# Linear attention with RMS norm and a mish feed-forward on one core: the start in halves and pairs, activation tables loaded at named places, steps placed anew

## The chip, the core and the metric

The kernel runs on one core of one Trainium2 chip. A core has a matrix engine (TensorE, PE in the profile; its weight loads are PEld), VectorE (DVE), ScalarE (ACT), GpSimd (POOL) and SyncE (SP), which work side by side, each on its own queue of instructions in order, and 16 DMA engines. SP issues nearly all loads, POOL most stores. The metric is the time of the whole program on the device, in microseconds (us), lower being better.

## The reference

q, k and v have 8 batches, 8 heads, 576 rows and 64 columns per head; x has 4608 rows of 512 columns.

```
kv  = einsum('bhsd,bhde->...', k, v)      # k^T v, 64 x 64 for each batch and head
out = einsum('bhsd,bhde->bhse', q, kv)
x   = out / sqrt(mean(out*out, -1) + 1e-6) * g_norm     # per row and head
h   = x @ w_in                             # 512 -> 2048
g   = h * tanh(log(1 + exp(h)))            # mish
res = g @ w_out                            # 2048 -> 512, fp32
```

w_in and w_out come in as 64-bit floats.

## The kernel before, in words

*Words and splits.* A unit j of w_in (two blocks of 256 columns, all 512 rows, 1 MB as 64-bit words) is loaded as pairs of 32-bit words by two DMAs, turned to fp32 by one ScalarE instruction (`scale`, L225) and three VectorE instructions (`join`, L220 to L222), and split into a high part, rounded to fp32r (`blocks`, ScalarE, L214), and a low part, the rest (VectorE, L215). A product of two such numbers takes three matmuls: high x high, high x low, low x high. x is split the same way. Each unit later gives differences of its blocks (`diff`), which are split too (`sums`) and stored (`store`), for a scheme with 7 block products in place of 8 (`group`, from L646).

*Tiles and slots.* The 4608 rows are nine tiles of 512. Part 1 makes h and g tile by tile, and stores g in DRAM; part 2 multiplies g by w_out. The order of part 1 is a row of numbered slots. A slot holds one product on TensorE, and behind it the steps that are due. Tile 0 has slots 0 to 31 and is multiplied in plain form (`whole_group`, L703: slots 0 to 3 use the first half of x's 512 columns, x0.0, kept in pages pa0 and pa1, slots 4 to 7 the second half, x0.1, in pb0 and pb1; two units of w_in each eight slots). Tiles 1 and 2 have slots 32 to 87, 12 matmuls of 256 columns each (L725); from slot 88 two tiles go together, 6 matmuls of 512 columns a slot (L735). Part 2 starts at about 434 us (L1256, L1106, L1111).

*Steps and places.* All else is in named steps: `w2.join` is the join of unit 2, `x0.1.rstd` the inverse root of tile 0's second half, `k5.v1` the load of v for the second half of the heads of batch 5, `k5.mul1` its k^T v product, `k5.keep1` the copy of that out of PSUM, `f1.0.0` a form of tile 1's x. The table `WHEN` gives each step its place as a number: a whole number t means behind the product of slot t, numbers below 0 come before slot 0, in their order. Nothing else sets the order: every engine's queue gets its instructions in that order, and waits are added where data or a buffer demand them. A step's place thus sets its order on its engines, not its time.

*Tile 0's attention* (the start). `kv.a` and `kv.b` load k and v of batch 0 (heads 0 to 3, heads 4 to 7), `rows.a` and `rows.b` the rows of q for the same heads, `rows.c` those of tile 1. Then for u = 0, 1 (four heads each): TensorE turns q (`transpose`, L484), ScalarE copies it out (`turned`, L495, L497), TensorE projects it on k^T v (`project`, L511), ScalarE squares (`square`, L517, L520), TensorE sums the squares over the head's 64 columns (`sums`, L534), ScalarE takes Ln and Exp (`rstd`, L547, L548), VectorE multiplies (`normalize`, L571), and `whole.u` splits the result. Each step handles two pairs of heads (1024 elements a partition) in one go, in one two-bank PSUM tile for u = 0. The first k^T v (`kv_first_product`, L389) writes the results of all pairs of heads straight, so it uses two of the four 64 x 64 quadrants of the array; later batches (`kv_product`, L400) use four, and `kv_keep` then swaps halves of the odd pairs back with two VectorE copies.

*Buffers.* w0, w4 and w7 share one room (w64): the load of w4 waits until w0's join has read it, and what follows on SP waits with it. v has one buffer per half batch (vm), k two: a load of v waits until the product before it has ended. wd (the differences) and x2 (PSUM) have one buffer as well.

*Tables.* ScalarE evaluates Ln, Exp and Mish from a loaded table; a function that is not in the current one makes the compiler put an ACT_TABLE_LOAD before it. `table.exp` (a set that holds Ln and Exp) and `table.mish` are explicit loads; `WHEN` has them at 139.787 and 110.923, so at the start Ln and Exp load a table each. For tiles 1 to 8, `rstd` loads the joint set itself, and the next mish loads its own.

Of the kernel before, what the change touches and what calls it, by code (L numbers as in the profile page):

```python
# [8 lines left out]
F32 = mybir.dt.float32  # L9
# [15 lines left out]
    "kv.a": -58.068, "constants": -56.889, "rows.a": -56.704, "w1.load": -56.033, "kv.mul.a": -55.141, "kv.b": -54.793,  # L25
# [98 lines left out]
def linear_attention_rms_mish_ffn(  # L124
# [140 lines left out]
    def weight_in(j, place):  # L265
# [9 lines left out]
        def scale():  # L275
            st["x"] = ring(j - (NF2 - 2), F32, True)[:, 0:PAGE] if j >= NF2 - 2 else page(f"wfa{j}", F32, True)
            scale_words(st["x"], st["w"])

        def join():
            join_words(st["x"], st["w"])  # L280
# [1074 lines left out]
```

## Time and profile before

| What | Value |
|---|---|
| three timed runs, median (lowest to highest) | 794.69 us (794.43 to 795.37) |
| the profiled execution's own time | 794.12 us |
| its span, first to last instruction | 792.3 us |
| TensorE busy | 772.8 us (98%) |
| VectorE busy | 601.9 us (76%) |
| ScalarE busy | 461.4 us (58%) |
| HBM read and written | 105.64 MB and 58.20 MB |

In the views of the trace, a row of the timeline gives start and duration in us, engine, line, operation, output and inputs, a count, and in brackets how long the engine was idle before it and what it waited for. `x72` at an fp32 matmul of the program counts its records, two for each. A row of the windows gives a stretch, its length, for each engine the busy time and in brackets the number of instructions that began in it (TensorE, its weight loads, VectorE, ScalarE, GpSimd), the granted clock of TensorE, the mean busy share of the DMA engines, and the GB/s that they moved. Matmuls are pipelined and their ends are modelled.

### The profile page before, as it was taken

What the parts mean: (1) busy time and instruction counts of PE and PEld (TensorE: products, weight loads), DVE (VectorE), ACT (ScalarE), POOL (GpSimd) and SP (SyncE); (2) the same over time, 40 slices, a digit from 0 to 9 for tenths busy, and PEclk for the clock granted to TensorE, in tenths of its full rate; (3) what the DMA queues carried; (4) which work ended last, traced back from release to release, by engine and by line L of the source; (5) the groups of instructions that cost most, each with busy time, mean ns of one, the idle gap of its engine ahead of it and who ended that gap; (6) DMA issues with size and microseconds to landing.
All of it is one profiled execution on the core that took longest, in us unless ns stands there. A gap on an engine that the chain in (4) does not pass through costs nothing.

```text
span 792.3 us, 13807 instructions
## 1 busy us (share of the span) xinstructions
PE 772.8 (98%) x5456; PEld 654.8 (83%) x5456; DVE 601.9 (76%) x713; ACT 461.4 (58%) x661; POOL 112.3 (14%) x179
## 2 busy tenths in 40 slices
PE   5799999999999999999999999999999999999997
PEld 4477899898878777888888988888888888888886
DVE  1888859488776986876467988888888888888885
ACT  4878566757666786566567644444444444444442
POOL 1013324232332323212111000000000000000000
PEclk9999999999999999999999999999999999999999
DMA  9997788789897768776847924444444444444412
GB/s 275 280 329 238 267 263 297 254 280 329 292 339 253 256 233 294 248 267 232 281 157 244 328 81 149 138 140 138 141 138 137 136 136 133 134 133 133 134 27 54
DMA packets 97969, 164.76 MB, mean 208 GB/s; under 512 B 15728, under 2 KB 62960, under 8 KB 97904
## 3 DMA queue, kind: packets, MB, share of 16 engines
q1 hardware_dynamic: 84304, 115.56, 46.5%
q0 software_dynamic: 13504, 48.24, 16.2%
q8 instruction: 43, 0.70, 0.4%
q14 instruction: 22, 0.18, 0.1%
q10 hardware_dynamic: 96, 0.07, 0.0%
HBM read 105.64 MB, written 58.20 MB: 207 GB/s over the span
## 4 chain that ended last, share of the span: by engine, by line
PE 92%; DMA 2%; DVE 2%; SPq 1%; ACT 1%; issue 1%; DVEq 0%
PE a L735 16%; PE a L1106 16%; PE bc L1106 12%; PE bc L735 12%; PE a L1111 8%; PE bc L1111 6%; PE a L725 6%; PE bc L725 4%; PE q L1256 3%; PE x L511 2%; PE bc L703 2%; PE a L703 2%; PE s L400 2%; SPq L434 1%; PE ss L541 1%; DMA vm<-in_v_dram 1%
## 5 line engine op out<-in xcount | busy, mean ns | idle before, releaser
L770 DVE TENSOR_TENSOR ula<-bc,ula 128x512 f32<-128x512 f32 x32 | 22.0, 686 | 39.6 <-ACT ur L665 15.4
L211 ACT ACTIVATE ur<-ur 128x1024 f32<-128x1024 f32 x32 | 33.9, 1059 | 25.3 <-DVE ur L770 25.1
L472 POOL COPY qs<-qs 32x1024 f32<-32x1024 f32 x28 | 33.0, 1180 | 43.4 <-DMA qs<-in_q_dram 39.6
L735 PE MATMUL a<-wfa,wfb 128*128 128x512 f32 x144 | 36.9, 391 | 0.0
L735 PE MATMUL bc<-wfa,tr 128*128 128x512 f32 x144 | 36.7, 390 | 0.0
L735 PE MATMUL bc<-wfc,wfb 128*128 128x512 f32 x144 | 36.7, 390 | 0.0
L214 ACT CAST wfc<-wfb 128x1024 fp32r<-128x1024 f32 x23 | 24.0, 1050 | 20.9 <-PE a L1111 11.6
L214 ACT CAST wfa<-g 128x1024 fp32r<-128x1024 f32 (+1 forms) x24 | 23.8, 998 | 19.4 <-PE a L1111 7.8
L215 DVE TENSOR_TENSOR wfa<-g,wfa 128x1024 fp32r<-128x1024 f32 (+1 forms) x24 | 27.5, 1154 | 9.1 <-ACT wfa L214 9.1
L665 ACT COPY ur<-a 128x512 f32<-128x512 f32 x32 | 18.8, 586 | 26.7 <-PE a L735 20.5
L735 PE MATMUL a<-pc,wfb 128*128 128x512 f32 x96 | 33.8, 393 | 0.1
L735 PE MATMUL a<-wfc,tr 128*128 128x512 f32 x96 | 33.8, 393 | 0.0
L735 PE MATMUL bc<-pa,wfb 128*128 128x512 f32 x96 | 33.7, 392 | 0.0
L735 PE MATMUL a<-pb,tr 128*128 128x512 f32 x96 | 33.7, 392 | 0.0
L214 ACT CAST wfa<-wfb 128x1024 fp32r<-128x1024 f32 x19 | 19.9, 1052 | 21.5 <-PE a L1111 15.5
L735 PEld LDWEIGHTS bc<-wfa,tr 128*128 128x128 f32 x144 | 26.9, 188 | 6.4 <-issue 0.8
L735 PEld LDWEIGHTS a<-wfa,wfb 128*128 128x128 f32 x144 | 26.8, 188 | 6.5 <-ACT tr L214 0.8
L211 ACT ACTIVATE ula<-ula 128x512 f32<-128x512 f32 x32 | 20.2, 631 | 19.9 <-DVE ula L770 19.8
L735 PEld LDWEIGHTS bc<-wfc,wfb 128*128 128x128 f32 x144 | 26.9, 188 | 5.7
L1161 DVE TENSOR_TENSOR ur<-ow 128x1024 f32<-128x1024 f32 x16 | 19.6, 1225 | 14.4 <-ACT ow L1158 14.3
L215 DVE TENSOR_TENSOR wfa<-wfb,wfa 128x1024 fp32r<-128x1024 f32 x19 | 23.1, 1221 | 8.9 <-ACT wfa L214 8.9
L770 DVE TENSOR_TENSOR ur<-bc,ur 128x512 f32<-128x512 f32 x32 | 21.9, 684 | 9.7 <-ACT ula L211 4.2
(574 smaller groups left out, 2479.0 us busy)
## 6 DMA issues: line engine op xcount, KB each, us to landing
gp<-ur POOLq DMA_DIRECT2D x24, 512.0 KB, 4.9
g<-gp SPq DMA_DIRECT2D x12, 1024.0 KB
wfb<-gp SPq DMA_DIRECT2D x12, 1024.0 KB
w<-in_moe_w_out_dram SPq DMA_DIRECT2D x16, 512.0 KB
km<-in_k_dram SPq DMA_DIRECT2D x14, 576.0 KB
vm<-in_v_dram SPq DMA_DIRECT2D x14, 576.0 KB
gp<-ula POOLq DMA_DIRECT2D x24, 256.0 KB, 3.9
gp<-ulb POOLq DMA_DIRECT2D x24, 256.0 KB, 3.7
```

The costliest lines, as they stand in the source:

```text
L211: nc.scalar.activation(o, i, AF.Mish)
L214: nc.scalar.copy(hi, src)
L215: nc.vector.tensor_sub(lo, src, hi.bitcast(F32))
L472: nc.gpsimd.tensor_copy(t[(i + 1) * R:(i + 2) * R, :, 0:R], t[i * R:(i + 1) * R, :, R:])
L703: nc.tensor.matmul(banks[m], w[:, a, kc, :], xf[b][:, kc], start=r == kc == s == 0, stop=(r == kc == 1 and s == 2), skip_group_check=True,)
L725: nc.tensor.matmul(bank[:, jj * TH:(jj + 1) * TH], w[:, a, kc, :], xf[b][:, kc], start=first and jj == kc == s == 0, stop=(kc == 1 and s = ...
L735: nc.tensor.matmul(bank, w[:, a, kc, :], xf[b][:, kc], start=first and kc == s == 0, stop=(kc == 1 and s == 2), skip_group_check=True,)
L770: nc.vector.tensor_add(o, bank_view(st, block, bank), o)
L1106: nc.tensor.matmul(halves(bank), gf[0][:, c], wo_form(c, right), start=first and c == 0, stop=False, skip_group_check=True,)
L1111: nc.tensor.matmul(halves(bank)[:, 0], gf[1][:, c], wo_form(c, right)[:, 0], start=False, stop=c == NF2 - 1, skip_group_check=True)
L1161: nc.vector.tensor_add(st["o"].rearrange("p r (c n) -> p (r c) n", c=2), a[:, :, 0], a[:, :, 1])
L1256: nc.tensor.matmul(banks[b][:, h], gf[a][:, c], wo_form(2 * n + c, right)[:, d], start=n == c == s == h == 0, stop=last_one, skip_group_ch ...
```

## The change

The start is cut finer and every step has a new place.

- Units 0, 1 and 2 of w_in are scaled, joined and split in halves (one of two column blocks each), so each of these steps is two; a half needs one of the unit's two DMAs.
- Tile 0's attention goes by pairs of heads: every step but rstd is there twice (512 elements a partition). Projections use the PSUM banks bc, which rotate; high and low parts are steps of their own. rstd does Ln, Exp for the first pair, then Ln, Exp for the second.
- The first k^T v uses `kv_product`, four quadrants, and `kv_keep` with its two VectorE copies.
- The joint Ln/Exp table is loaded by the first instruction on ScalarE; mish's table is loaded at the end of x0.1's rstd and at the end of the rstd of each of tiles 1 to 8. The steps table.exp and table.mish are gone.
- `WHEN` is new throughout. On SP, the order at the start was kv.a, rows.a, w1, kv.b, rows.b, w0, w2, k1.k0, k1.v0, w4, w3, k1.k1, rows.c; it becomes kv.a, rows.a, w1, w0, rows.b, kv.b, w2, k1.k0, k1.v0, w4, w3, rows.c, w5, k1.k1.

The diff, cut to its core:

```diff
 WHEN = {
...
-    "k5.mul0": 70.827, "k5.v1": 74.729, "k5.mul1": 81.43, "k6.mul0": 85.133, "k6.v1": 88.135, "k6.mul1": 90.167,
-    "k4.mul0": 56.221, "k4.mul1": 62.614, "k3.mul0": 39.547, "k3.mul1": 44.249, "table.mish": 110.923, "table.exp": 139.787,
+    "k5.mul0": 78.799, "k5.v1": 78.831, "k5.mul1": 82.324, "k6.mul0": 87.671, "k6.v1": 89.911, "k6.mul1": 91.127,
+    "k4.mul0": 58.613, "k4.mul1": 62.687, "k3.mul0": 40.104, "k3.mul1": 44.815,
+    "rows.a": -54.973, "w1.load": -52.565, "w0.load": -50.279, "rows.b": -49.677, "kv.b": -49.025, "w2.load": -47.673,
+    "x0.0.square0": -46.31, "w1.scale1": -42.097, "w0.scale0": -40.175, "x0.0.project1": -39.243, "x0.0.square1": -37.584,
+    "kv.mul.b": -28.683, "x0.1.project0": -19.47, "w2.scale1": -15.726, "w0.blocks1": -14.997, "w2.blocks0": -12.839,
+    "x0.1.rstd": -11.645, "x0.1.high0": -10.975, "x0.1.low1": -4.102, "k1.mul0": 3.676, "x1.0.transpose": 9.14,
...
-        def scale():
+        def scale(h=None):
+            if "x" not in st:
...
+            scale_words(st["x"][:, half_of(h)], st["w"][:, half_of(h)])
...
-    def kv_first_product(n):
...
-    def kv_first_keep(n):
-        nc.scalar.copy(kvt[0][:, n], kvps[:, 0, n, :])
...
+    def root(r, mean):
+        nc.scalar.activation(r, mean, AF.Ln, bias=eps, scale=1.0 / D)
+        nc.scalar.activation(r, r, AF.Exp, scale=-0.5)
+
+    def first_steps(u):
...
+        def turned(a):
+            if "q" not in st:
+                st["q"] = turned_q if u else att.tile([P, 2, T], F32, name="fh")
+            nc.scalar.copy(st["q"][:, a], st["x2"][:, a])
+
+        def project(a):
+            st["x"][a] = bank_new("bc")
+            for o in range(2):
+                nc.tensor.matmul(st["x"][a][half(o)], kvt[0][half(o), 2 * u + a], st["q"][half(o), a], start=True, stop=True)
...
+        def rstd():
+            for a in range(2):
+                root(st["s"][:, a], st["ss"][a])
+            if u == 1:
+                nc.scalar.preload_act_table_set("mish")
...
+        def high(a):
+            nc.scalar.copy(two(WHOLE[u][0])[:, a], x_part(0, u)[:, a])
+
+        def low(a):
+            hi, lo = (two(name)[:, a] for name in WHOLE[u])
+            nc.vector.tensor_sub(lo, x_part(0, u)[:, a], hi.bitcast(F32))
...
             nc.scalar.preload_act_table_set("natural_log_exp_and_others")
-            nc.scalar.activation(r, ss[j], AF.Ln, bias=eps, scale=1.0 / D)
-            nc.scalar.activation(r, r, AF.Exp, scale=-0.5)
+            root(r, ss[j])
+            nc.scalar.preload_act_table_set("mish")
...
     def k_product(b, n):
-        kt, vt = (staged.pop((name, b, n)) for name in "kv")
-        staged[b, n] = kv_product(b, n, [(kt[:, a], vt[:, a]) for a in range(2)])
+        if b == 0:
+            ts = [[kv0[name][:, hp] if hp + 1 < NKC else kv0[name, NKC] for name in "kv"] for hp in (2 * n, 2 * n + 1)]
+        else:
...
+        staged[b, n] = kv_product(b, n, ts)
...
+    nc.scalar.preload_act_table_set("natural_log_exp_and_others")
     for name, f in begin:
```

In this cut the entries of `WHEN` stand regrouped; all of them have new numbers.

More of the change, by code (lines that the diff above doesn't have):

```diff
@@ L24 @@
 WHEN = {
-    "kv.a": -58.068, "constants": -56.889, "rows.a": -56.704, "w1.load": -56.033, "kv.mul.a": -55.141, "kv.b": -54.793,
[93 rows of a table removed]
+    "constants": -56.889, "kv.a": -55.729, "rows.a": -54.973, "kv.mul.a": -53.46, "x0.0.transpose1": -53.308,
[98 rows of a table added]
 }
@@ L273, in load, with half_of, join @@
             st["w"] = load_words(place(), srcs, 2)
-        def scale():
[L276 to L280, printed above, removed]
+        def half_of(h):
+            return slice(None) if h is None else slice(h * FORM, (h + 1) * FORM)
+        def scale(h=None):
+            if "x" not in st:
+                st["x"] = ring(j - (NF2 - 2), F32, True)[:, 0:PAGE] if j >= NF2 - 2 else page(f"wfa{j}", F32, True)
+            scale_words(st["x"][:, half_of(h)], st["w"][:, half_of(h)])
+        def join(h=None):
+            join_words(st["x"][:, half_of(h)], st["w"][:, half_of(h)])
         def parts(t, src):
@@ L284, in parts, with blocks @@
             split(hi, lo, src)
-        def blocks():
-            wb[j] = wfp.tile([P, 4 * FORM], F32R, name=f"wfb{j}")
-            parts(forms(wb[j]), st["x"].rearrange("p (b n) -> p b n", b=4))
+        def blocks(h=None):
+            if j not in wb:
+                wb[j] = wfp.tile([P, 4 * FORM], F32R, name=f"wfb{j}")
+            n = slice(0, 4) if h is None else slice(2 * h, 2 * h + 2)
+            parts(forms(wb[j])[:, n], st["x"].rearrange("p (b n) -> p b n", b=4)[:, n])
         def differences():
@@ L412, in kv_keep @@
         if b < T32:
-            nc.scalar.copy(kvx[:, n], odd)
+            if b:
+                nc.scalar.copy(kvx[:, n], odd)
             for o in range(2):
@@ L454, in linear_attention_rms_mish_ffn, with transpose, square, sums @@
     SQUARES = {SINGLE + 1: ("xa", "xh")}
+    def root(r, mean):
+        nc.scalar.activation(r, mean, AF.Ln, bias=eps, scale=1.0 / D)
+        nc.scalar.activation(r, r, AF.Exp, scale=-0.5)
+    def first_steps(u):
+        st = {"ps": [None] * 2, "x": [None] * 2, "ss": [None] * 2}
+        def transpose(a):
+            if "x2" not in st:
+                st["x2"] = ps_t.tile([P, 2, T], F32, name="x2")
+            h = 4 * u + 2 * a
+            for c in range(TR):
+                nc.tensor.transpose(st["x2"][:, a, c * P:(c + 1) * P], rows[0][:, c, h * D:(h + 2) * D], ident)
+        def turned(a):
[6 more added lines that the diff above has]
+                nc.tensor.matmul(st["x"][a][half(o)], kvt[0][half(o), 2 * u + a], st["q"][half(o), a], start=True, stop=True)
+        def square(a):
+            if "s" not in st:
+                st["s"] = att.tile([P, 2, T], F32, name=("fa", "fh")[u])
+            nc.scalar.square(st["s"][:, a], st["x"][a])
+        def sums(a):
+            st["ss"][a] = bank_new("a") if u == 0 else ps_t.tile([P, T], F32, name="ss") if a == 0 else kvps.rearrange("p b n d -> p (b n d)")
+            nc.tensor.matmul(st["ss"][a], ones, st["s"][:, a], start=True, stop=True)
+        def rstd():
[3 more added lines that the diff above has]
+                nc.scalar.preload_act_table_set("mish")
+        def normalize(a):
+            nc.vector.scalar_tensor_tensor(x_part(0, u)[:, a], st["x"][a], gcol, st["s"][:, a], ALU.mult, ALU.mult)
+        def high(a):
[3 more added lines that the diff above has]
+            nc.vector.tensor_sub(lo, x_part(0, u)[:, a], hi.bitcast(F32))
+        return {f.__name__: f for f in (transpose, turned, project, square, sums, rstd, normalize, high, low)}
     def unit_steps(j, u):
@@ L475, in transpose @@
             if j < T32:
-                if j == 0 and u == 1:
-                    ps = [ps_t.tile([P, T], F32, name="ss"), bank_new("bc")]
-                else:
-                    x2 = ps_t.tile([P, 2, T], F32, name="x2")
-                    ps = [x2[:, a] for a in range(2)]
+                st["ps"] = ps_t.tile([P, 2, T], F32, name="x2")
                 for a in range(2):
@@ L483, in transpose @@
                     for c in range(TR):
-                        nc.tensor.transpose(ps[a][:, c * P:(c + 1) * P], rows[j][:, c, h * D:(h + 2) * D], ident)
-                st["ps"] = ps if j == 0 and u == 1 else x2
+                        nc.tensor.transpose(st["ps"][:, a, c * P:(c + 1) * P], rows[j][:, c, h * D:(h + 2) * D], ident)
                 return
@@ L491, in turned @@
         def turned():
-            t = st["q"] = turned_q if j == 0 and u == 1 else att.tile([P, 2, T], F32, name="fh")
-            if j == 0 and u == 1:
-                for a in range(2):
-                    nc.scalar.copy(t[:, a], st["ps"][a])
-            else:
-                nc.scalar.copy(t, st["ps"])
-        def project():
-            if j == 0 and u == 1:
-                st["x"] = [bank_new("bc") for _ in range(2)]
-            else:
-                x2 = st["x2"] = ps_t.tile([P, 2, T], F32, name="x2")
-                st["x"] = [x2[:, a] for a in range(2)]
+            st["q"] = att.tile([P, 2, T], F32, name="fh")
+            nc.scalar.copy(st["q"], st["ps"])
+        def project():
+            st["x"] = ps_t.tile([P, 2, T], F32, name="x2")
             for b, _, c in segments(j):
@@ L510, in project @@
                         r = half(o, turned)
-                        nc.tensor.matmul(st["x"][a][half(o), c], kv[r], st["q"][r, a, c], start=True, stop=True)
+                        nc.tensor.matmul(st["x"][half(o), a, c], kv[r], st["q"][r, a, c], start=True, stop=True)
         def square():
-            st["s"] = spare(j, SQUARES.get(j, ("fa", "fh"))[u])
-            sq[j, u] = st["s"]
-            if "x2" in st:
-                nc.scalar.square(st["s"], st["x2"])
-            else:
-                for a in range(2):
-                    nc.scalar.square(st["s"][:, a], st["x"][a])
+            sq[j, u] = spare(j, SQUARES.get(j, ("fa", "fh"))[u])
+            nc.scalar.square(sq[j, u], st["x"])
         def scaled():
@@ L524, in scaled @@
             if j <= T32:
-                nc.scalar.activation(o, st["x2"], AF.Identity, scale=gcol)
+                nc.scalar.activation(o, st["x"], AF.Identity, scale=gcol)
             else:
-                nc.vector.tensor_scalar(o, st["x2"], gcol, None, ALU.mult)
+                nc.vector.tensor_scalar(o, st["x"], gcol, None, ALU.mult)
         def sums():
-            if j == 0:
-                st["ss"] = []
-                for a in range(2):
-                    ps = bank_new("a") if u == 0 else ps_t.tile([P, T], F32, name="ss") if a == 0 else kvps.rearrange("p b n d -> p (b n d)")
-                    nc.tensor.matmul(ps, ones, st["s"][:, a], start=True, stop=True)
-                    st["ss"].append(ps)
-                return
             ss[j] = ps_t.tile([P, T], F32, name="ss")
@@ L543, in rstd @@
         def rstd():
-            if j == 0:
-                r = st["r"] = st["s"]
-                for a in range(2):
-                    nc.scalar.activation(r[:, a], st["ss"][a], AF.Ln, bias=eps, scale=1.0 / D)
-                nc.scalar.activation(r, r, AF.Exp, scale=-0.5)
-                return
             r = st["r"] = att.tile([P, T], F32, name="fl")
             nc.scalar.preload_act_table_set("natural_log_exp_and_others")
-            nc.scalar.activation(r, ss[j], AF.Ln, bias=eps, scale=1.0 / D)
-            nc.scalar.activation(r, r, AF.Exp, scale=-0.5)
+            root(r, ss[j])
+            nc.scalar.preload_act_table_set("mish")
         def keep():
@@ L616, in x_form @@
             nc.scalar.copy(hi, src)
-    def x_whole(r):
-        split(*(two(name) for name in WHOLE[r]), x_part(0, r))
     def bank_new(name):
@@ L804, in k_product @@
     def k_product(b, n):
-        kt, vt = (staged.pop((name, b, n)) for name in "kv")
-        staged[b, n] = kv_product(b, n, [(kt[:, a], vt[:, a]) for a in range(2)])
+        if b == 0:
+            ts = [[kv0[name][:, hp] if hp + 1 < NKC else kv0[name, NKC] for name in "kv"] for hp in (2 * n, 2 * n + 1)]
+        else:
+            kt, vt = (staged.pop((name, b, n)) for name in "kv")
+            ts = [(kt[:, a], vt[:, a]) for a in range(2)]
+        staged[b, n] = kv_product(b, n, ts)
     def k_keep(b, n):
@@ L849, in linear_attention_rms_mish_ffn @@
     t1 = start(1)
-    begin = (
-        ("table.exp", lambda: nc.scalar.preload_act_table_set("natural_log_exp_and_others")),
+    firsts = [first_steps(u) for u in range(2)]
+    begin = [
         ("w0.load", None), ("rows.a", rows_first), ("kv.a", kv_rooms), ("w1.load", None), ("rows.b", rows_second),
@@ L854, in linear_attention_rms_mish_ffn @@
         ("w4.load", None), ("k1.k0", None), ("k1.v0", None),
-        ("w0.scale", None), ("w0.join", None), ("x0.0.transpose", None), ("x0.0.turned", None), ("w0.blocks", None),
-        ("kv.mul.a", lambda: kv_first_product(first)), ("kv.keep.a", lambda: kv_first_keep(first)),
-        ("w1.scale", None), ("x0.0.project", None), ("x0.0.square", None), ("w1.join", None),
-        ("x0.1.transpose", None), ("x0.0.sums", None), ("x0.1.turned", None), ("w1.blocks", None),
-        ("x0.0.rstd", None), ("kv.mul.b", lambda: kv_first_product(rest)), ("kv.keep.b", lambda: kv_first_keep(rest)),
-        ("x0.0.normalize", None), ("x0.1.project", None), ("w2.scale", None), ("whole.0", lambda: x_whole(0)),
-        ("x0.1.square", None), ("w3.scale", None), ("rows.c", rows_next),
-    )
+        ("kv.mul.a", lambda: k_product(0, 0)), ("kv.keep.a", lambda: k_keep(0, 0)),
+    ]
+    FIRST_STEPS = ("transpose", "turned", "project", "square", "sums", "rstd", "normalize", "high", "low")
+    begin += [(f"x0.0.{n}{a}", None) for n in FIRST_STEPS[:4] for a in range(2)]
+    begin += [(f"w0.{n}{h}", None) for n in ("scale", "join", "blocks") for h in range(2)]
+    begin += [("kv.mul.b", lambda: k_product(0, 1)), ("kv.keep.b", lambda: k_keep(0, 1))]
+    begin += [(f"x0.0.{n}{a}", None) for n in FIRST_STEPS[4:] for a in range(2) if n != "rstd"]
+    begin.insert(len(begin) - 6, ("x0.0.rstd", None))
+    begin += [(f"x0.1.{n}{a}", None) for n in FIRST_STEPS[:4] for a in range(2)]
+    begin += [(f"w1.{n}{h}", None) for n in ("scale", "join", "blocks") for h in range(2)]
+    begin += [(f"w2.scale{h}", None) for h in range(2)] + [("w3.scale", None), ("rows.c", rows_next)]
     early = {name: n - len(begin) for n, (name, _) in enumerate(begin)}
+    nc.scalar.preload_act_table_set("natural_log_exp_and_others")
     for name, f in begin:
@@ L866, in linear_attention_rms_mish_ffn @@
             step(name, early[name], f)
[L867 to L875 removed]
+    for u in range(2):
+        for n, name in enumerate(FIRST_STEPS):
+            for a in range(2) if name != "rstd" else ("",):
+                key = f"x0.{u}.{name}{a}"
+                step(key, early.get(key, 0.01 + 0.01 * n), lambda u=u, name=name, a=a: firsts[u][name](*(() if a == "" else (a,))))
     STEPS = ("load", "scale", "join", "blocks", "diff", "sums", "store")
[L878 removed]
+    made = {0: (-80, -25, -24, -20), 1: (), 2: (0, 0, 0.5, 0.6), 3: (0, 0, 3, 5), 4: (0, 6, 6.1, 8), 5: (1, 9, 9.1, 11), 6: (4, 13, 13.1, 15), 7: (8, 16, 16.1, 18)}
     for j in range(NF2):
[L880 removed]
+        t = (1.5, 21, 23, 25, t1 + 6, t1 + 8, t1 + 13, t1 + 15)[j]
         for n, name in enumerate(STEPS):
[L882 to L886 removed]
+            for h in range(2) if j < 3 and 0 < n < 4 else (None,):
+                key = f"w{j}.{name}" + ("" if h is None else str(h))
+                when = early[key] if key in early else made[j][n] if n < 4 else (t, t + 1, t + 0.5)[n - 4]
+                step(key, when, lambda j=j, n=n, h=h: conv[j][n](*(() if h is None else (h,))))
     for b, t, loads, made in (
```

28 lines of the change are left out of this document (1 added, 27 removed), and 191 rows, old and new, of the table WHEN.

## The prediction

> **What bounds the kernel now.** I read the page first, for the share of each engine, then the waits of TensorE, then the windows and the order of time of the first 45 us.
>
> ```profile
> span 792.3 us, 13807 instructions
> PE 772.8 (98%) x5456; PEld 654.8 (83%) x5456; DVE 601.9 (76%) x713; ACT 461.4 (58%) x661; POOL 112.3 (14%) x179
> PE   5799999999999999999999999999999999999997
> ```
>
> TensorE is busy for 98% of the span; its idle time lies in the first two of the 40 slices and at the very end. Its waits after the first product of the feed-forward part (28 to 50 us), and then all from 50 to 440 us (from 440 us on the view is empty), are these:
>
> ```profile
> PE x L484 <- DMA qs<-in_q_dram: 1.1, 1, 1.1
> PE a L703 <- ACT wfb L214: 0.9, 1, 0.9
> PE a L703 <- DVE pb L215: 0.5, 1, 0.5
> PE a L703 <- DVE wfb L215: 0.5, 1, 0.5
> ```
> ```profile
> PE s L400 <- DMA vm<-in_v_dram: 0.8, 1, 0.8
> ```
>
> So the work on TensorE behind the first product is fixed, and the change can win only by starting that work sooner and by taking out these waits, some 3.8 us of them. The rows of the start, in order of time, and four of the chain of waits (start, us):
>
> ```profile
> 6.42 4.09 PE L389 MATMUL s<-wfb,wfb 64*64 64x64 f32 x72 [6.42 <-DMA wfb<-in_v_dram]
> ...
> 12.86 1.14 ACT L225 ACTIVATE wfa<-wfb 128x1024 f32<-128x1024 f32 x1 [0.28 <-DMA wfb<-in_moe_w_in_dram]
> 14.76 1.23 DVE L221 SCALAR_TENSOR_TENSOR wfa<-wfb,wfa 128x1024 uint32<-128x1024 uint32 x1
> ...
> 21.83 0.59 ACT L495 COPY wfa<-ss 128x512 f32<-128x512 f32 x1
> ...
> 22.47 1.93 PE L511 MATMUL bc<-wfa,kv 64*64 64x512 f32 x8 [1.46 <-ACT wfa L495]
> ...
> 26.38 1.02 PE L534 MATMUL s<-fh,ones 128*128 128x512 f32 x2
> ...
> 27.25 0.92 SPq L234 DMA_DIRECT2D w<-in_moe_w_in_dram  x2
> ...
> 28.31 0.73 PE L703 MATMUL a<-pa,wfb 128*128 128x512 f32 x2 [0.91 <-ACT wfb L214]
> ...
> 29.57 2.56 PE L703 MATMUL a<-pa,wfb 128*128 128x512 f32 x10 [0.52 <-DVE wfb L215]
> ...
> 37.05 2.79 PE L703 MATMUL a<-pb,wfb 128*128 128x512 f32 x11 [0.54 <-DVE pb L215]
> ...
> 39.69 0.48 DVE L415 COPY kv<-ss 64x64 f32<-64x64 f32 x2
> ```
> ```profile
> 45.37 0.77 PE x L484 x5
> ...
> 73.93 2.72 PE a L703 x12
> ...
> 86.25 1.43 PE a L725 x12
> ...
> 175.80 7.42 DMA vm<-in_v_dram
> ```
>
> The first tile's attention ends on TensorE at 26.38 + 1.02 = 27.4 us. The first product starts at 28.31 and stalls until 29.57, since w_in's first unit is converted whole and late. The second half of the tile (slot 4, which reads pb) runs from 37.05, one matmul earlier in effect, so I count it from 36.8. The transposes of tile 1 wait for its q rows until 45.37 (45.3 below).
>
> **The change, part by part.** Sums are made against the profiled run: 794.12 us with its span of 792.3; the median of the three timed runs is 794.69, so 0.57 is added at the end.
>
> *DMA order.* These rows give the rates of all DMA (the last figure, GB/s) and the sizes:
>
> ```profile
> 0.00:10.00 10.00, 3.58 (x67) 3.61 (x69) 0.00 (x0) 1.28 (x1) 2.62 (x15) 1.00 0.85 232
> 10.00:20.00 10.00, 7.68 (x103) 4.61 (x101) 3.14 (x3) 7.61 (x9) 0.00 (x0) 1.00 1.10 318
> 25.00:30.00 5.00, 3.15 (x8) 1.36 (x9) 4.97 (x5) 4.65 (x6) 0.00 (x0) 1.00 0.53 173
> 30.00:35.00 5.00, 5.00 (x90) 4.00 (x89) 3.98 (x5) 3.50 (x5) 0.00 (x0) 1.00 1.06 350
> ```
> ```profile
> wfb<-in_moe_w_in_dram SPq DMA_DIRECT2D x10, 512.0 KB
> wfb<-in_q_dram SPq DMA_DIRECT2D x8, 128.0 KB
> wfb<-in_k_dram SPq DMA_DIRECT2D x1, 576.0 KB
> wfb<-in_k_dram SPq DMA_DIRECT2D x1, 288.0 KB
> ```
>
> w0.load now goes ahead of rows.b and kv.b on SP's queue. Up to and with kv.b that is 2x576 + 4x128 + 2x512 + 2x512 + 4x128 + 4x288 KB = 5.50 MB. The rates give 2.32 MB by 10 us and 5.50 MB by 20.0 us. How much a landing lags behind this count shows at w1: 2.75 MB, moved by 11.4 us, waited for until 12.86, so 1.5 us. kv.b lands at 21.5 (bounds 20.0 without lag, 22.5 with one more us); before, its product ran at 17.7 without a wait. This move takes back most of what the change could win: kv.mul.b waits on TensorE for kv.b, and x0.1's projections and the first product of the feed-forward part stand behind it in the same queue.
>
> *First k^T v on quadrants.* Its 72 records took 4.09 us at the start and 2.31 later, the same number on four quadrants (L400) 1.28:
>
> ```profile
> 17.00:20.00 3.00, 2.31 (x72) 2.18 (x72) 1.00 1.06 333
> 33.40:34.80 1.40, 1.28 (x72) 1.14 (x72) 1.00 1.06 353
> ```
>
> The first of the two products is hidden (q's rows and x0.0's chain come before kv.b anyway). The second is on the path, 1.28 from 21.5 to 22.8. kv.keep.b then costs a copy on ScalarE and two on VectorE (0.48, row L415), 0.3 of it on the path.
>
> *Attention by pairs.* x0.1's two projections now start at 23.1 and take 1.93 (L511), the last square 0.6 (as the 512-wide copy at L495), the last sum 1.02 (L534): TensorE is free at 26.6. VectorE must by then have made w0's first half and x0.0's low parts. From the landing of w0's first half (3.27 MB, so 13.0 + 1.5, and 0.6 for its scale) at 15.1 it has three halved joins (about 0.45 + 0.7 + 0.7 each, half of the L221 row and its neighbours with a fixed share), seven 512-wide differences or products and the keep copies: 15.1 + 5.5 + 4.7 = 25.3. That lies under 26.6. So the products run from 26.6 with no wait of 0.9 or 0.5.
>
> *Second half.* Slots 0 to 3 take 4 x 1.36 (half of the 2.72 row) and k1.mul0 1.28: slot 4 can start at 33.3. Its x must come through Ln, Exp, Ln, Exp, which stand on ScalarE behind w2.scale1, w0.blocks1 and w2.blocks0, so from about 28 us: 2.7 us (0.69 + 0.64 twice, rows below), then the mish load 1.28, high 0.6, low 0.7: 33.3. TensorE and the chain meet there; I take 33.4.
>
> ```profile
> 63.90 1.28 ACT L551 ACT_TABLE_LOAD   x1
> 65.20 0.69 ACT L552 ACTIVATE fl<-ss,eps 128x512 f32<-128x512 f32 x1
> 65.92 0.64 ACT L553 ACTIVATE fl<-fl 128x512 f32<-128x512 f32 x1
> ```
>
> Gain here 36.8 - 33.4 = **3.4** (2.4 with kv.b at 22.5; 4.3 with kv.b at 20.0, where VectorE's 25.3 takes over). *Tables*: of the first 45 us' loads, grouped by line, these four go, 5.1 us of ScalarE's queue, against some 0.13 for each halved instruction there (0.59 twice instead of 1.05):
>
> ```profile
> L547 ACT ACT_TABLE_LOAD x2 | 2.6, 1283 | 0.0
> L548 ACT ACT_TABLE_LOAD x2 | 2.6, 1283 | 0.0
> ```
>
> The mish load now stands on x0.1's path, ahead of its high parts, and not behind it. The Trainium skill (ScalarE: Activation LUTs, What ACT_TABLE_LOAD costs) has 2.66 us for a switch, a drain included; here Ln starts 0.02 after the load at L551 has taken its 1.28. By the page slot 4 would be 1.4 later and the gain 2.0.
>
> *Tile 1's q rows.* w4.load had to wait for w0's join until 27.25, and DMA ran at 173 GB/s for 5 us instead of 350: a hole of 0.88 MB or 2.5 us. w0's join now ends near 20.6 (the three halved joins above), w3.load and rows.c stand behind w4.load and move up with it, so the hole closes; and k1.k1 (0.59 MB, 1.7 us) goes behind the rows: 45.3 - 4.2 = 41.1. It in turn stands behind w5.load, which waits for w2's join (about 31); its product is not due before slot 14, past 48. TensorE asks at 33.4 + 6 x 1.36 = 41.6. The wait of 1.1 goes; if only one of the two shifts comes true, the rows land near 43.6 and 0.9 is lost. I take **+0.8**, nearer to the hole's row.
>
> *VectorE's extra work.* Halves cost a second fixed share (three joins 0.45 each, five low parts 0.14) and the keep copies 0.96: about 3.0 us, behind VectorE's idle time before 14 us and 8 us of gaps between 30 and 70. Where that cover is gone,
>
> ```profile
> 70.00:80.00 10.00, 9.86 (x15) 1.00 0.67 208
> ```
>
> each us late is one of TensorE's. Bounds 0 and 1.0; I take **-0.4**.
>
> *Places anew.* Loads of v have one buffer, so each starts when the product before it ends. k4, k5 and k6 now have their products closer: k5.mul0 to mul1 has 4 products of 1.43 and 1.28 = 7.0 us; k4's pair 8.2; k5.mul1 to k6.mul0 8.5; k6's pair 7.7. One such load took 7.42, and starts 1.36 after its product's first matmul: 8.8 us. Were all like that, the waits would be 1.8 + 0.6 + 0.3 + 1.1 = 3.8 against 0.8 now; but of 14 loads just one was waited for. Bounds +0.8 and -3.0; I take **-0.3**. The other new places move work of engines on which TensorE doesn't wait.
>
> Sum: 3.4 + 0.8 - 0.4 - 0.3 = 3.5. 794.12 - 3.5 = 790.6, on the scale of the median 791.2.
>
> **The rivals.** *TensorE slow again.* The first 72 records took 4.09 us, the same number later 2.31, though the clock column (the third figure from the end) reads 1.00 in both stretches: the array began slow. On ScalarE w0.scale0 waits for its landing (14.5) with x0.0's second square behind it, so that square ends at 15.7 and the last sum at 16.7; from there to kv.mul.b (21.5) TensorE has transposes alone; the longest gap in the rows before is 1.46. If it falls back, some 4.1 us run 1.7 times slower, 1.7 us lost: 792.9. For it: the length of the gap. Against it: the array stayed fast with waits of 1 to 1.5 us throughout. The Trainium skill (TensorE: Matmul & The Clock Gate, Part 1) puts the fallback at a full idle window of about 3.4 us and (Part 4: PE-mode transpose) doesn't count transposes as busy; by it this is likelier than the rows alone say, and no run here shows it yet.
>
> *DMA sets the pace as before*: kv.b at 22.5 and the rows at 43.6, then 1.0 + 1.7 of the gain are gone: 793.9. For it: both start stages are at 318 to 350 GB/s, and no byte is saved. Against it: the hole is real.
>
> *The single v buffer*, the slower side: the waits are new ones of TensorE itself, in slots 58 to 92. It eats the gain from loads of about 7.5 us on; with 8.2 us each the five tight places (k3's pair with 9.1 joins) wait 2.6 + 1.4 + 1.1 + 1.9 + 0.5 = 7.5, 6.4 more than I took beside the 0.8 saved: 797.6. For it: the row of 7.42. Against it: one wait in 14.
>
> *The tables don't hold*: Ln and Exp load their own again, now eight times instead of four, x0.1's four on the path: 5.1 + its share of x0.0's: 797. Against it: between L552 and L553, behind the same preload, no load stands.
>
> **How the numbers follow.** Forecast 0.58; slow array 0.15; DMA 0.13; v buffer 0.12; tables 0.02. What can be told from no change is 0.2%, 1.6 us: faster is below 793.1. The forecast and two thirds of the slow array are faster, 0.68; the rest of that and DMA, with the milder v buffer, 0.20; the rest slower, 0.12. Range: 788.5 (4.3 + 1.1 + 0.8) up to 795.0, which leaves out the slower cases.
>
> **What would show it.** First product near 26.6 with no wait behind it; slot 4 near 33.4; x1.0's transposes unwaited near 41.6; two table loads before 40 us; L389's work at 1.3 us on quadrants; waits on vm as listed. I am wrong if the first product is after 28, or if waits of over 1 us stand between 130 and 210 us.

## The result and the profile after

The changed kernel takes 800.86 us (median of 5 runs, 800.01 to 803.33), the kernel before, run between them, 794.69 us (792.61 to 796.6). The ratio is 1.0081, 95% interval 1.0055 to 1.0107: slower by some 6 us. Its profiled execution took 800.01 us, with a span of 798.2 us. The forecast of 791.2 us and its range up to 795.0 were wrong, and in direction.

From the page of the changed kernel, as for the kernel before:

```profile
span 798.2 us, 13836 instructions
PE 775.7 (97%) x5456; PEld 653.6 (82%) x5456; DVE 604.8 (76%) x731; ACT 452.6 (57%) x666; POOL 113.3 (14%) x179
PE   4899999999999999999999999999999999999997
PEclk9899999999999999999999999999999999999999
```

The second digit of the clock row is 8: in the second slice of 20 us the array was not at full speed throughout. Before, it read 9 there. The start in order of time:

```profile
16.80 1.79 PE L470 MATMUL x<-ident,wfb 128*128 128x128 f32 x8
20.36 0.39 PE L403 MATMUL s<-wfb,wfb 64*64 64x64 f32 x4 [1.77 <-DMA wfb<-in_v_dram]
22.57 0.37 PE L403 MATMUL ss<-pc,pc 64*64 64x64 f32 x2 [1.82 <-DMA pc<-in_v_dram]
...
24.89 3.12 PE L480 MATMUL bc<-wfa,kv 64*64 64x512 f32 x8
27.94 1.13 PE L489 MATMUL ss<-fh,ones 128*128 128x512 f32 x2
28.91 1.02 PE L489 MATMUL s<-fh,ones 128*128 128x512 f32 x2
29.36 2.84 PE L718 MATMUL a<-pa,wfb 128*128 128x512 f32 x10
```

TensorE has k and v of the second heads at 22.57, and the two projections behind them take 3.12 us, not 1.93. The windows of these 10 us show why:

```profile
17.09:20.50 3.41, 1.40 (x11) 0.80 (x10) 3.27 (x7) 3.38 (x7) 0.00 (x0) 1.00 0.97 292
20.50:23.92 3.42, 1.60 (x54) 1.41 (x55) 2.98 (x5) 1.54 (x3) 0.00 (x0) 0.50 0.99 354
23.92:27.33 3.41, 3.28 (x34) 1.40 (x32) 2.43 (x6) 1.72 (x4) 0.00 (x0) 0.50 1.06 381
```

The granted clock is half for two stretches of 3.41 us, right behind one in which TensorE was busy for 1.40 us, mostly with transposes. The first product starts at 29.36 (before 28.31) without a stall behind it.

Starts of some slots (first matmul of the slot's product, us), the later columns from experiments below. So that the traces can be compared, each is shifted to have its first k^T v at 6.45 us; that moves the column of the old late places by 0.51, the others by 0.07 or less:

| Slot | before | after | old late places | change's late places in before | extra products, batch 5 earlier |
|---|---|---|---|---|---|
| 4 | 36.15 | 36.50 | 35.22 | 37.01 | 34.19 |
| 44 | 110.49 | 109.08 | 107.80 | 112.70 | 106.77 |
| 88 | 187.56 | 189.38 | 185.93 | 194.11 | 184.67 |
| 112 | 227.52 | 233.69 | 225.92 | 238.05 | 224.63 |
| 172 | 321.15 | 327.02 | 319.59 | 331.44 | 319.10 |

At slot 44 the changed kernel is 1.4 us ahead, at slot 172 it is 5.9 behind, and it stays so to the end. So 7.3 us are lost between these two slots. A lead of 1.4 us is not much for single traces: in the four kernels of experiments 4 and 5, which have the changed kernel's program up to slot 64, slot 44 starts at 109.05 to 111.64. The loss is well above that spread. TensorE's waits from 36 to 450 us, which held a total of 2.4 before:

```profile
PE s L403 <- DMA vm<-in_v_dram: 2.6, 2, 1.8
PE a L750 <- ACT ula L667: 1.2, 2, 0.9
PE x L551 <- DVE x L562: 0.8, 1, 0.8
PE ss L569 <- ACT fh L555: 0.6, 1, 0.6
PE a L750 <- DVE ur L785: 0.2, 1, 0.2
PE x L551 <- ACT xa L555: 0.2, 1, 0.2
```

All six lie behind slot 44; the view names 5.6 us there, against 0.8 before. The same stretch from slot 44 to 172, in one window of each kernel, first before, then after:

```profile
110.49:321.15 210.66, 209.67 (x1837) 173.15 (x1834) 161.06 (x204) 144.37 (x215) 67.01 (x93) 1.00 0.82 277
```
```profile
109.08:327.02 217.94, 212.29 (x1840) 173.14 (x1833) 160.47 (x201) 139.39 (x212) 67.41 (x91) 1.00 0.81 265
```

Nearly the same count of matmul records (1837 and 1840) at the same clock: TensorE's idle time grew from 1.0 to 5.7 us. The other 2.6 us stand as busy time; ends of matmuls are modelled, so a part of them may belong to the same waits, which this view can't show. They stay without a name.

Two of the chains behind the waits. At 144 us ScalarE's square (L555) and VectorE's scaled copy (L562) read the same PSUM tile; the new places have the copy first, VectorE reaches it late, and the square and TensorE's sums stand behind it:

```profile
143.65 1.27 DVE L562 TENSOR_SCALAR x<-x,gcol 128x1024 f32<-128x1024 f32 x1
...
144.96 1.02 ACT L555 ACTIVATE fh<-x 128x1024 f32<-128x1024 f32 x1 [2.27 <-DVE x L562]
...
146.03 1.05 PE L569 MATMUL ss<-fh,sel 128*32 128x512 f32 x4 [0.61 <-ACT fh L555]
```

The square starts 0.04 us after the copy's end. The Trainium skill (PSUM — Partial Sum Buffer, PSUM bank collisions raise a hardware error) has any two engines kept apart on one bank, reads too; by that rule the order of the two steps is a wait, and the trace agrees.

And at 187 us the first product of batch 6 needs a v that was requested only when batch 5's second product had ended, 9.07 us earlier:

```profile
178.25 0.37 SPq L377 DMA_DIRECT2D vm<-in_v_dram  x1
...
187.32 0.27 PE L403 MATMUL s<-vm,km 64*64 64x64 f32 x2 [1.78 <-DMA vm<-in_v_dram]
```

### The profile page after: what moved, and what is told of

It reads as the page before. It is cut to its first block, busy times and chain, and to the rows that moved or that the text cites. A ratio compares the mean times of both kernels' runs of the same rounds, so it can differ in the third digit from the quotient of the medians.

```text
span 798.2 us, 13836 instructions
## 1 busy us (share of the span) xinstructions
PE 775.7 (97%) x5456; PEld 653.6 (82%) x5456; DVE 604.8 (76%) x731; ACT 452.6 (57%) x666; POOL 113.3 (14%) x179
## 4 chain that ended last, share of the span: by engine, by line
PE 74%; DVE 2%; DMA 2%; issue 1%; ACT 1%; SPq 0%; DVEq 0%; ACTq 0%
PE a L1124 16%; PE a L750 14%; PE bc L1124 12%; PE bc L750 11%; PE a L1129 8%; PE bc L1129 6%; PE q L1274 3%; DMA vm<-in_v_dram 2%; PE a L740 2%; PE bc L740 1%; PE x L551 1%; PE s L403 1%; PE ss L569 1%; DVE wfa L632 0%; DVE x L623 0%
## 5 line engine op out<-in xcount | busy, mean ns | idle before, releaser
L785 DVE TENSOR_TENSOR ur<-a,ur 128x512 f32<-128x512 f32 x32 | 22.0, 686 | 12.3 <-PE a L750 7.1
```

The lines of the kernel that those rows point to most:

```text
L785: nc.vector.tensor_add(o, bank_view(st, block, bank), o)
```

## The experiments

Each time is the median of its runs, each ratio is to the kernel before, run between them. "Late places" are those whose place before was 44 or more. Slot numbers are those of the table above.

**1. The change with the old late places, and the old kernel with the new ones.** The first tells the start from the rest, the second is its mirror. Two lines stand for all of them:

```diff
 WHEN = {
-    "k5.mul1": 82.324, "k6.mul0": 87.671, "x3.1.scaled": 65.221, "x3.1.square": 65.454,
+    "k5.mul1": 81.43, "k6.mul0": 85.133, "x3.1.scaled": 62.804, "x3.1.square": 62.631,
...
```

> The changed kernel, but every step whose place in the kernel before is at slot 44 or later has that old place again; the start, the halves, the pairs and the tables stay as changed. Theory (late places): slot 31 stands 1.2 us earlier than before, and the 7.2 us that are lost between slots 44 and 172 come from the new places there; so 794.7 - 1.2 = 793.5 us, and TensorE's waits for vm are 0.8 us again. Rival (the earlier start itself makes later transfers collide, whatever the places): 799 to 801 us.

> The kernel before, with only the places from slot 44 on taken from the changed kernel; nothing of the start is changed. Theory (late places): 794.7 + 7 = 801.5 us, with the waits on vm (about 2.6 us) and the four others between 130 and 300 us as in the changed kernel. Rival (the start makes them): 794 to 795 us.

The change with the old late places: 793.65 us, 0.9986 (0.9969 to 1.0004). The old kernel with the new ones: 802.23 us, 1.0083 (1.006 to 1.0106). So the places from slot 44 on carry the whole loss, in either kernel, and what is left of the change is worth 1 us that can't be told from none. In the old kernel with the new places, TensorE waits 3.2 us on v and 2.7 us on ScalarE and VectorE from 50 us on. The waits of the first one from 36 to 450 us:

```profile
PE s L410 <- DMA vm<-in_v_dram: 1.3, 1, 1.3
PE a L747 <- ACT ur L687: 0.3, 1, 0.3
```

The five rows of waits on VectorE and ScalarE (3.0 us in all) are gone but for 0.3 us, and so is one of the two on v.

**2. The array kept busy ahead of kv.b**, in the changed kernel and in the one with the old late places. The three matmuls compute nothing that is used.

```diff
+    def warm(n):
+        d = ps_t.tile([P, T], F32, name="ss")
+        for _ in range(n):
+            nc.tensor.matmul(d, ones, rows[0][:, 0], start=True, stop=True)
+    at(-31.5, lambda: warm(3))      # ahead of kv.mul.b
```

> The changed kernel with three extra matmuls (ones times q rows, 128x512 fp32, into a PSUM bank that nobody reads) on TensorE between x0.1's transposes and kv.mul.b, where it waits for kv.b: they compute nothing that is used. Theory (slow array): the granted clock no longer falls to 0.50 between 20.5 and 27.3 us, kv.mul.b and x0.1's projections run at full speed, the first product starts near 27.6 instead of 29.36 and slot 4 near 34.5 instead of 36.5; total 800.9 - 2.0 = 798.9 us. Rival (the chain is set by kv.b and by ScalarE alone, the clock costs nothing): 800.5 to 801 us, slot 4 at 36.5.

> The changed start with the three unused matmuls of the run with fillers, and the old places from slot 44 on. If both theories hold and the parts add: 794.7 - 1.2 - 2.0 = 791.5 us. If later waits take up what the start wins: 793.5 us.

The changed kernel: 801.83 us, 1.0072 (1.0049 to 1.0095), no gain. With the old late places: 792.37 us, 0.9961 (0.9946 to 0.9976), which beats both kernels, though its interval overlaps the 0.9969 to 1.0004 without the added products. In both traces the clock never fell again, but it rose only at 22 us, so the start was no faster: the first product comes at 30.04 and 29.80, against 29.36 in the changed kernel. Until then the clock has no record and the windows read 1.00; that it was half is seen from the first pair's projection, 1.07 us in the changed kernel's trace and here, with the old late places:

```profile
11.22 1.97 PE L487 MATMUL bc<-fh,kv 64*64 64x512 f32 x4 [0.68 <-ACT fh L482]
```

**3. The tables alone**, in the kernel before.

```diff
+    nc.scalar.preload_act_table_set("natural_log_exp_and_others")   # first on ScalarE
...
     nc.scalar.activation(r, r, AF.Exp, scale=-0.5)
+    nc.scalar.preload_act_table_set("mish")
```

> The kernel before with one part of the change alone: the Ln/Exp table is loaded at the start, the Mish table right after each rstd; everything else, the places too, is as before. Theory that the table loads stood in the way (four loads of 1.28 us fewer on ScalarE before the first attention slot, and the load ahead of slot 4 gone): 1.0 to 1.5 us faster than before, 793.2 to 793.7, slot 4 starting that much earlier. Theory that ScalarE's loads were hidden there behind the DMA and TensorE: within 0.4 us of before, 794.3 to 795.1.

795.51 us, 0.9996 (0.9979 to 1.0014); the span of the trace is 1.1 us shorter than before's, with slot 4 no earlier (36.27) and slot 172 at 319.87 (shifted as in the table). The interval holds both theories: not settled.

**4. The two chains attacked**, in the changed kernel: v loaded earlier (with the copies out of PSUM behind the moved products, eight places in all), the square ahead of the copy (four places), and both.

```diff
-    "k5.mul0": 78.799, "k5.v1": 78.831, "k5.mul1": 82.324, "k6.v0": 83.026, "k7.mul0": 106.308, "k7.v1": 108.437,
+    "k5.mul0": 72.0, "k5.v1": 72.1, "k5.mul1": 79.5, "k6.v0": 80.7, "k7.mul0": 105.6, "k7.v1": 105.65,
-    "x3.1.square": 65.454, "x4.0.square": 67.489, "x5.0.square": 90.93, "x6.0.square": 109.599,
+    "x3.1.square": 65.15, "x4.0.square": 67.4, "x5.0.square": 90.4, "x6.0.square": 108.2,
```

> The changed kernel with nine places of the k^T v steps of tiles 5 to 7 moved: both products that read a v buffer come earlier, and the next v load right behind the product that frees the buffer, so that each load is issued 6 to 9 us ahead of its product. Theory that the two stalls of TensorE on late v loads (1.85 and 0.87 us in the changed kernel's trace) set the end: 2.0 to 2.7 us faster than the changed kernel, 798.2 to 798.9. Theory that each stall only covers the next one, ScalarE's evictions that come late right behind it: within 0.8 us of the changed kernel, 800.1 to 801.6.

> The changed kernel with four places moved: ScalarE's square of the projected rows of tiles 3 to 6 is issued just ahead of VectorE's scaled copy of the same rows, and not just behind it. Theory that ScalarE is held by the square that waits for VectorE's copy (2.27 us and 1.21 us waits in the changed kernel's trace, with 1.2 + 0.41 + 0.44 us of TensorE's stalls behind them): 1.2 to 2.0 us faster than the changed kernel, 798.9 to 799.7. Theory that VectorE is late in any order and the wait goes to the copy and what follows it: within 0.6 us of the changed kernel, 800.3 to 801.5.

> Both sets of moved places together, 13 places of the changed kernel's. Theory that the stalls in the middle add up and each is its own: 3.2 to 4.7 us faster than the changed kernel, 796.2 to 797.7, with about half of the 7.2 us that the old late places gave back. Theory that the stalls replace one another: no better than the better of the two alone, 798.2 or more.

No gain in any: 807.53 us, 1.0142 (1.0115 to 1.017) with v earlier; 802.62, 1.0077 (1.005 to 1.0104) with the square first; 810.68, 1.0185 (1.0151 to 1.022) with both. The kernel before took 796.24 us between these runs, so the ratios are the ones to compare: the square first is as the changed kernel (1.0081), as its second theory had it, and the other two are slower than it. With the square first, TensorE's wait on it went, but VectorE's copy (L568) now waited for the square, 2.0 us twice and 1.0 once between 100 and 300 us, and two waits of TensorE on VectorE came:

```profile
PE x L557 <- DVE fl L543: 1.4, 1, 1.4
PE x L557 <- DVE wfa L568: 1.2, 1, 1.2
```

With v earlier, the wait on v fell from 2.6 to 0.3 us, and these came first:

```profile
PE bc L745 <- DVE ula L790: 3.2, 1, 3.2
PE bc L745 <- ACT ur L677: 2.3, 1, 2.3
```

The order of time shows how. SyncE, VectorE and TensorE of that kernel:

```profile
162.87 0.37 SPq L382 DMA_DIRECT2D vm<-in_v_dram  x1
...
166.21 1.90 SPq L592 DMA_DIRECT2D fa<-rd  x2
```
```profile
176.05 1.22 DVE L596 TENSOR_TENSOR x<-x,fa 128x1024 f32<-128x1024 f32 x1 [9.78 <-DMA fa<-rd]
```
```profile
183.10 2.79 PE L745 MATMUL bc<-pa,tr 128*128 128x256 f32 x12 [3.18 <-DVE ula L790]
```

VectorE stands still for 9.78 us over a reload of the inverse roots (`spread`, fa from rd), issued at 166.21; the weight steps and then the eviction that TensorE waits for (L790) queue behind it. In the changed kernel the same reload is issued at 158.18. My reading was that SyncE itself had been held, by a v load at the head of its queue which waits for the one buffer: between 154.21 and 162.87 SyncE issues nothing, and its own waits name the product before (L408) for that load, 8.6 us.

**5. The same with the v loads of batches 5 to 7 on GpSimd's queue.**

```diff
-        nc.sync.dma_start(t, bass.AP(src.tensor, src.offset, [[9 * D, P], [2 * S * D, 2], [1, 9 * D]]))
+        (nc.gpsimd if name == "v" and b >= 5 else nc.sync).dma_start(t, bass.AP(src.tensor, src.offset, [[9 * D, P], [2 * S * D, 2], [1, 9 * D]]))
```

> The nine moved places of k^T v steps of tiles 5 to 7, which came out at 807.5 us, with the v loads of batches 5 to 7 issued from GpSimd's queue and not from SyncE's. Theory that an early v load waits for the one v buffer at the head of SyncE's queue and holds the reloads of the turned rows behind it, so that VectorE stands still (9.78 us in that trace) and TensorE behind VectorE: the loss goes, 798 to 801, and the 9.78 us gap of VectorE with it. Theory that the earlier products themselves crowd ScalarE and VectorE: no better than 805. A loss of its own is possible, since GpSimd's stores then wait behind the load.

800.9 us, 1.0069 (1.0049 to 1.0089): some 6 us are back (0.0073 of the ratio), the reload is issued at 160.13, and VectorE's wait on it is this:

```profile
169.00 1.23 DVE L596 TENSOR_TENSOR x<-x,fa 128x1024 f32<-128x1024 f32 x1 [0.51 <-DMA fa<-rd]
```

So it was the held queue. But the kernel is no better than the changed one: TensorE waits 2.4 us on v in two other places (at 110 and 197 us) and 1.3 us on ScalarE's L672.

**6. The late places split by kind**: the changed kernel with the old ones of the k^T v steps, or of all other steps. In each, a copy of k^T v comes ahead of a tile that still reads an earlier batch in the same room (in the first, batch 4's before tile 3; in the second, batch 7's before tile 6), so some heads of that tile are multiplied with a later batch's k^T v; the work is the same, its dependences are not quite.

```diff
-    "k5.mul0": 78.799, "k5.mul1": 82.324,
+    "k5.mul0": 70.827, "k5.mul1": 81.43,
```

> The changed kernel with the late places (before's number 44 and up) of the k^T v steps alone, loads, products and copies, taken from the kernel before; the late places of all other steps stay the changed kernel's. Theory that the places of the k^T v products (v loads of up to 9 us in one buffer) cost the 7 us behind slot 44: 5 to 7 us faster than the changed kernel, 793.9 to 795.9, with no waits on v above 1.5 us. Theory that it is the order of the other steps on ScalarE and VectorE, on which TensorE's PSUM banks wait: 0 to 2 us faster, 798.9 to 800.9. Theory that either set must fit the other, so that any mixture is bad: slower than the changed kernel, over 802.

> The other half of the same split: the changed kernel with the late places of all steps but k^T v taken from the kernel before. Theory of the k^T v places: 0 to 2 us faster than the changed kernel, 798.9 to 800.9. Theory of the other steps' order: 5 to 7 us faster, 793.9 to 795.9. Theory that any mixture is bad: over 802.

803.03 us, 1.0105 (1.0084 to 1.0126), and 810.55 us, 1.0195 (1.0178 to 1.0211). Both fit the third theory, and neither kind carries the loss alone: the second mixture is worse than either whole order, the first can't be told from the changed kernel (1.0081, 1.0055 to 1.0107). Waits on v became 4.7 us in the first, 2.1 in the second, beside 5.6 us of the matmuls at L746 on evictions.

**7. One load of v, later and earlier**, in the kernel of 792.37 us, which had one wait on v left, 1.4 us.

```diff
-    "k5.mul1": 81.43, "k5.keep1": 81.508,
+    "k5.mul1": 82.43, "k5.keep1": 82.63,
```
```diff
-    "k5.mul1": 81.43, "k5.keep1": 81.508,
+    "k5.mul1": 80.43, "k5.keep1": 80.5,
```

> The kernel of the earlier run at 792.37 us (the changed kernel with the three added products that compute nothing that is used, and with before's late places) with the second k^T v product of batch 5 and the copy behind it placed one slot later. Its trace had one wait on v left, 1.4 us at that product; one slot is 1.43 us. If the wait is TensorE's own, 0.9 to 1.4 us faster than that kernel, ratio to before near 0.9945. If another load or copy takes its place: no change, ratio near 0.9961.

> The mirror of the run at 796.92 us. That run's trace corrects my reading: the one wait on v left in the kernel at 792.37 us (1.4 us) stood at the first product of batch 6, and moving batch 5's second product one slot later made the load that waits behind it start 2.85 us later and the wait 3.1 us, with 3.41 us at half clock behind it. Here that product and the copy behind it are placed one slot earlier. If the wait is set by when the load of v can start: it shrinks to 0 to 0.3 us and the time to 790.7 to 791.5, ratio near 0.9945. If the earlier product crowds ScalarE or holds SyncE: 792.4 or more.

Later: 796.92 us, 1.0015 (1.0002 to 1.0029). I had read the wait one product off; the run became a test of the price instead. The load starts at 178.31, not 175.46, the wait at batch 6's first product grows to 3.1 us, and slot 92 comes 3.8 us later. The wait and the clock in three equal windows:

```profile
PE s L410 <- DMA vm<-in_v_dram: 3.1, 1, 3.1
```
```profile
179.67:183.08 3.41, 3.06 (x26) 2.85 (x24) 3.31 (x4) 2.62 (x4) 0.00 (x0) 1.00 0.98 279
183.08:186.50 3.42, 0.64 (x41) 0.67 (x45) 1.75 (x2) 2.23 (x3) 0.00 (x0) 0.99 1.02 211
186.50:189.91 3.41, 3.41 (x55) 3.29 (x47) 0.00 (x0) 1.45 (x4) 2.76 (x4) 0.51 0.52 167
```

A wait that left TensorE 0.64 us of work in a window was followed by a window at half clock, which costs another 1.7 us (half of 3.41).

Earlier: 792.34 us, 0.997 (0.9954 to 0.9986), the same as without. The wait on v halved, and those on VectorE and ScalarE behind it grew from 0.2 to 0.7:

```profile
PE s L410 <- DMA vm<-in_v_dram: 0.7, 1, 0.7
PE a L757 <- DVE ur L792: 0.4, 1, 0.4
PE a L757 <- ACT ula L674: 0.3, 1, 0.3
```

In its trace the clock rose at 10.0 us and never fell, so it shows the start as predicted, without the half clock:

```profile
23.72 1.93 PE L487 MATMUL bc<-wfa,kv 64*64 64x512 f32 x8 [0.22 <-ACT kv L418]
25.58 1.12 PE L496 MATMUL ss<-fh,ones 128*128 128x512 f32 x2
26.55 1.02 PE L496 MATMUL s<-fh,ones 128*128 128x512 f32 x2
27.00 3.33 PE L725 MATMUL a<-pa,wfb 128*128 128x512 f32 x12
```

**8. The array kept busy from 2 us on.** Eighteen small products (`ones` by `ones`, 128 columns) before the first k^T v, five of the others in the gap; again nothing uses them.

```diff
+    at(-54.5, lambda: warm_early(18))
-    at(-31.5, lambda: warm(3))
+    at(-31.5, lambda: warm(5))
```

> The kernel at 792.37 us with 18 small products more on TensorE before the first k^T v, from 2 us on, and five in place of three in the gap ahead of kv.b; none of them computes anything that is used. Theory that the array's clock took part of the gain at the start: full clock from the first k^T v (1.3 us and not 2.0) to the end, first product near 27.5 to 28.3 and slot 4 near 34.7 in the trace, 1 to 2 us faster than the kernel without them, 790.4 to 791.4. Theory that DMA sets that stretch (k and v of the second heads land at 22.5 whatever TensorE does): slot 4 near 36.5 to 37, 792 to 793.

> Both of these edits together: by the two theories that expect a gain 789.0 to 790.2, ratio 0.992 to 0.994; if only one of them holds, 790.5 to 791.5; if neither, 792.4 or more.

> The changed kernel itself with the same 18 and five added products and its own places. If the half clock at the start cost it the 1 to 2 us that the first product came late, 798.9 to 799.9; if that is given back by the waits behind slot 44, which do not move, 800.5 to 802.

With the old late places 793.84 us, 0.998 (0.9968 to 0.9991); with batch 5 earlier too 793.82, 0.9978 (0.9966 to 0.999); in the changed kernel 800.96, 1.0061 (1.0038 to 1.0083). The clock was full from 7.5 us on at the latest, and the first product came at 27.8 to 27.9 in each, 1.5 us ahead of the changed kernel. But no time follows: by the intervals nothing is gained on 0.9961 and 1.0081. In the changed kernel the lead has gone by slot 44 (109.03 against 109.10, both as they stand in the traces), and the trace shows where: a wait on v that the changed kernel doesn't have there.

```profile
107.82 0.27 PE L403 MATMUL s<-vm,km 64*64 64x64 f32 x2 [1.33 <-DMA vm<-in_v_dram]
```

So most of what TensorE won at the start it lost again waiting for a load.

## Why the prediction was wrong, by its steps

**What bounds the kernel: half right.** TensorE sets the pace. But "the change can win only by starting that work sooner and by taking out these waits" looked at what the change takes away. With TensorE idle 1 us in 210, almost any new order can only add waits. Both signs of being wrong that the prediction named came: the first product after 28 (29.36) and a wait of over 1 us between 130 and 210 us (1.78 at 187).

**The sum.** In the two traces it reads 0.3 at slot 4 (3.4 predicted) + 1.1 for the q rows - 7.3 between slots 44 and 172 = -5.9, the difference of the spans. Of the 7.3, 1.8 are waits on v, 3.0 waits on ScalarE and VectorE, and some 2.5 have no name. Neither the 3.0 nor the 2.5 had a term.

**The step that failed** is the last sentence of "Places anew": "The other new places move work of engines on which TensorE doesn't wait." It put these places at nothing, and behind slot 44 TensorE waited 3.0 us on ScalarE and VectorE (five rows above), where it had waited for none before. An engine on which TensorE doesn't wait in the old order says nothing of a new order. Experiment 1 shows that the late places carry the loss; which of them is not settled and may have no answer, since experiments 4 to 6 only moved the waits or added to them.

**The single v buffer** (taken at -0.3, bounds +0.8 to -3.0, and the slower rival): right mechanism, term mis-sized. Waits on v rose from 0.8 to 2.6 us, -1.8, inside the bounds. The load took 9.07 us to its product, not 7.42 or 8.2. It hit one of the four places named (batch 5 to 6) and one that was not (batch 7). The rival's price of 797.6 is nearest to the result, but by this buffer alone it was not reached.

**DMA order**: kv.b at 21.5 was taken, 22.57 measured, past the upper bound of 22.5. **Quadrants**: 1.28 us taken, 2.2 measured, at half clock; 1.39 at full clock, in the first trace of experiment 8. **Slot 4**: 33.4 predicted, 36.50 measured; of the gain of 3.4, 0.3 came. The trace of experiment 7 in which the clock held, with kv.b at 22.24, has the first product at 27.00 (predicted 26.6) and slot 4 at 34.19. So the order of the start was read rightly; by that trace 0.8 us goes with kv.b, and 2.3 (36.50 - 34.19) with the clock and a kv.b that is 0.3 later still. The bound of 4.3 for an early kv.b does not follow from its own 25.3, which gives 1.3 more than 3.4, so 4.7; nothing hangs on it here.

**TensorE slow again** was a rival at 0.15, priced at 1.7: it happened in the changed kernel's trace, at the place named, in a window with little but transposes. The Trainium skill (TensorE: Matmul & The Clock Gate, Part 4: PE-mode transpose) doesn't count transposes as busy; the trace agrees, but can't tell it from a share of busy time that is too low, since the next window, with 1.60 us of k^T v, was followed by half clock too. It was priced at 1.7 us, against 2.3 at most; but in the changed kernel curing it won nothing (experiment 8). Of *DMA sets the pace*, kv.b came as late as that rival had it, the rows did not.

**Tile 1's q rows**: right. The transposes no longer wait: they start at 44.82, behind slot 9, while before they stood ahead of it and waited 1.1. With 0.3 from slot 4 and this 1.1 the lead of 1.4 at slot 44 is complete in this pair of traces, so they show no cost of **VectorE's extra work** (-0.4) there. **Tables**: they hold, and the load costs what L551 showed, here before a mish:

```profile
241.45 1.28 ACT L575 ACT_TABLE_LOAD   x1
242.75 1.06 ACT L216 ACTIVATE ur<-ur 128x1024 f32<-128x1024 f32 x1
```

The next instruction starts 0.02 after it; the 2.66 us of the Trainium skill (ScalarE: Activation LUTs, What ACT_TABLE_LOAD costs) isn't borne out.

## What to carry to other kernels

Where one engine is busy for 98%, price a new order by what it may add: ask of every moved step whether the busy engine's next buffer now stands behind it, and don't take old slack of the other engines as theirs in the new order. A load that waits for its buffer holds everything behind it on its queue (8.6 us on SyncE in experiment 4), so "earlier" can be worse. Change places in whole sets that fit each other: of the two mixtures of the old and the new order here, neither beat the worse of the two whole orders, and one was among the two slowest kernels (1.0195).

## What the runs showed of the hardware

The granted clock of TensorE changed at steps of 3.41 us whose phase differed from run to run: half-clock stretches ahead of the kernel's end were 3.41 or 6.83 us long, as the Trainium skill says of a free-running window (TensorE: Matmul & The Clock Gate, Part 1). Not by that section, which asks for an idle window: windows with 0.64 and with 1.40 us of TensorE's work in 3.41 were followed by half clock. When the clock first rose differed too. With the first k^T v on four quadrants (2.2 us at half clock) and no early products, its first record is at 9.7 to 10.3 us in 5 of 12 traces and at 17.8 to 22.9 in the others; with the two-quadrant form (4.09 us) it is at 10.4 to 12.2 in all three. That the shorter first burst makes the rise less sure is a guess from these few traces, not shown.
